# Splitting the last weight but one of a soft MoE into a whole part and two column halves, on one Trainium2 core

## The chip, the core and the metric

The kernel runs on one NeuronCore of a Trainium2 chip. Its engines are the tensor engine (PE, with its weight loads shown apart as PEld), the vector engine (DVE), the scalar engine (ACT), GpSimd (POOL) and the sync engine (SP); 16 DMA engines move data between HBM and the on-chip memory SBUF. Products land in PSUM, which has eight banks. The metric is the time of one execution on the device, in microseconds (us); smaller is better. The time given for a kernel is the median of several executions.

## What is computed

A masked attention over 4 batches, 8 heads, 768 positions and 64 values per head feeds a soft mixture of experts with 8 experts of 4 slots each. The reference, cut to what matters:

```python
scores = np.where(mask, q @ k.T / np.sqrt(64), -1e9)      # per batch and head
x = softmax(scores) @ v                                    # -> (3072, 512)
logits = x @ phi                                           # (3072, 32)
d = softmax(logits, axis=0)
slot_input = (d.T @ x).reshape(8, 4, 512)
for e in range(8):
    slot_out[e] = np.maximum(slot_input[e] @ w1[e], 0) @ w2[e]   # w1: 512x1024, w2: 1024x512
c = softmax(logits, axis=1)
out = c @ slot_out.reshape(32, 512)                        # (3072, 512) float32
```

Half of the heads see all earlier positions, the others the first 4 and the last 64.

## The kernel before

**Loads.** All inputs but three small pieces are loaded by DMAs that POOL issues and that cast float32 to bfloat16 on the way (the helper `dma`, lines 343 to 351; the instruction is at line 347). They go into one queue, q0 in the profile, one behind the other. The weights are called w0 to w15: w0 to w7 are the eight matrices of the first layer, w8 to w15 those of the second, one for each expert. Each is 2 MB as float32 and 1 MB as bfloat16. A matrix of the second layer lies in SBUF as 128 partitions times 8 rows (`fo`) of 512 columns. w8 to w13 arrive whole, in runs of four rows, 4096 bytes as bfloat16, for a partition. w14 and w15 (experts 6 and 7) go by `load_half` (line 395) in two column halves each, so that a run is one row of 256 columns, 512 bytes: w14 left, w15 left, w14 right, w15 right, in this order (lines 967 to 970). They land in memory that the attention has left: `pt` for w14, `qk` for w15, as `qk` for w11, `vx` for w12 and `xv` for w13 (lines 955 to 959).

**Attention.** Sixteen steps (4 batches of 4 pairs of heads) of score products (line 656), exponentials on ACT (line 726), masks on DVE (line 672), products with v (line 800), normalisation (line 824) and transposes; then logits and slot inputs.

**Experts.** `H` (line 1008) multiplies the slot inputs with the first layer, `HR` (line 1018) applies the ReLU, `TH` and `HE` (lines 1030 and 336) transpose. `w2_op` (line 1041) issues for one expert the products W2 (line 1046), one for each of the 8 rows `fo`, on a quarter of the PE array each; all experts add up in one PSUM bank. Experts 0 to 5 take all 512 columns at a time. For experts 6 and 7 the left 256 columns come first and the right 256 after them. Three products with zeros (`wait_zeros`, line 1061, called ZT0 and ZT1) stand between the two experts of a half and keep PE running.

**Output.** `SO.0` and `SO.1` (line 1104) evict the left and the right half of the experts' sum. The 3072 output rows are six groups `gi` of 512, each a tile of 128 partitions, 4 rows `r` and 512 columns. `out_tile` (line 1116) makes one product (OM, line 1121) and one eviction (OE, line 1129 on ACT or 1131 on DVE) for a group, an `r` and a range of columns; the eviction scales with `rrow`, the reciprocal of the row sums. The row sums are 12 small products for three groups at a time (`RW0` and `RW1`, line 1087), and DVE takes their reciprocal (line 1091). The twelve tiles of groups 0 to 2 are made in halves: all left halves as soon as `SO.0` is done, then all right halves after `SO.1`. The twelve tiles of groups 3 to 5 are made whole, after these.

**Stores.** `store` (line 1137, instruction at line 1140). Four stores of left halves go by POOL, on the queue of the loads, behind all of them: 128 KB, 384 KB, 512 KB and 512 KB. SP issues seven more on its own queue, q1: the right halves of group 0 in two pieces of 256 KB, those of groups 1 and 2 (512 KB each), and the three whole groups (1024 KB each).

**Order.** A planner (`Plan.run`, line 69) places all operations by estimated costs and by keys (due times), and the instructions are emitted in that order. What an operation costs in this plan, the DMAs' `took` of line 349 among it, decides the order on each engine and nothing else: at run time each engine goes through its own list and waits on semaphores.

```python
    for e in range(NE - NSPLIT):
        w2_op(e, 0, 2)
    whole = w2o[0]
    for c in range(2):
        for e in range(NE - NSPLIT, NE):
            w2_op(e, c, c + 1)
            if e == NE - 2:
                wait_zeros(f"ZT{c}", 3, kt + (29.5 + e if c else 22.5), w2o[c], c == 0)
```

Of the kernel before, what the change touches and what calls it, by code (L numbers as in the profile page):

```python
# [151 lines left out]
def pe(ns, n=1):  # L152
    occ = ns * n / 1000.0
    return {"PE": (occ, occ + 0.27)}
# [72 lines left out]
def kernel(  # L227
# [15 lines left out]
    B, H, S, D = q.shape  # L243
# [3 lines left out]
    NE, DM, F = moe_w1.shape  # L247
# [61 lines left out]
    def tr_bf(s, n):  # L309
# [19 lines left out]
    def on(eng, occ, late=0.18):  # L329
        return {eng: (occ, occ + late)}  # L330
# [12 lines left out]
    def dma(name, nbytes, buf, dst, src, deps=()):  # L343
        if len(chain) >= 8:
            deps = list(deps) + [chain[-8]]
        iss = pl.op("issue " + name, on("POOL", 0.645, 1.4), -100, deps=list(deps) + [fifo[0]],
                    acq=[buf] if buf else [], lead=1.3, emit=lambda o: nc.gpsimd.dma_start(dst(), src))  # L347
        fifo[0] = iss
        took = nbytes / (395000.0 if nbytes == 1 << 20 and name != "w0" else 423000.0)
        chain.append(pl.op("land " + name, {"DMA": (took, took + 1.85 + 0.05 * len(chain))}, -100, deps=[iss] + chain[-1:], lead=5.2))  # L350
        return chain[-1]

# [23 lines left out]
    NW, NSPLIT = 2 * NE, 2  # L376
    wbuf = [Buf("S8") for _ in range(NW)]
    wland = [None] * NW
    late_mem = {}
# [6 lines left out]
    def w_row(i, x):  # L386
        n = 2 if i < NE else 4
        return w_mem(i)[:, x // n, :].rearrange("p (a f) -> p a f", a=n)[:, x % n, :]

    def w_half(i, c):  # L390
        return late_mem[i]()[:, 2048 * c:2048 * (c + 1)].rearrange("p (a f) -> p a f", a=8)

    hland = {}

    def load_half(i, c, deps=()):
        src = moe_w2[i - NE].rearrange("(fi fo) d -> fi fo d", fo=8)[:, :, 256 * c:256 * (c + 1)]
        hland[i, c] = dma(f"w{i}.{c}", 1 << 20, None, lambda: w_half(i, c), src, deps=deps)

    def load_w(i, deps=()):
        if i == 0:  # L400
# [106 lines left out]
    for x in range(5):  # L507
# [26 lines left out]
    def phi_t2(o):  # L534
        for n in range(4):
# [14 lines left out]
    def load_tile(ti):  # L550

        tbuf[ti], tland[ti], p0 = Buf("S8"), [], 0
        for x, b, x0, x1 in TILES[ti]:
# [8 lines left out]
                  emit=lambda o, x=x: nc.gpsimd.tensor_copy(w_mem(0)[:, 0, KB * x:KB * (x + 1)],  # L562
                                                            w0f[:, KB * x:KB * (x + 1)])) for x in range(4)]
# [116 lines left out]
    for b in range(B):  # L680
        for n in range(4):
            p = 4 * b + n
# [4 lines left out]
            def emit_v2(o, n=n, tr=tr):  # L687
                t = tr_bf(tr.slot, 768)
                for j in range(6):
                    nc.tensor.transpose(t[:, 128 * j:128 * (j + 1)], vT[:, 6 * n + j, :], ident)  # L690

            a = pl.op(f"V2.{p}", pe(56, 6), k0 + 1.5, deps=evs("v", b, n), acq=[tr], rel=[VTb[b]],
                      emit=emit_v2, mode="full", mm=6)

            def emit_vb(o, b=b, n=n, tr=tr):
# [4 lines left out]
                           acq=[VBb[b]] if n == 0 else [], rel=[tr], emit=emit_vb)  # L700
            VFb[p] = Buf("VF")

            def emit_vf(o, b=b, n=n, p=p):
# [4 lines left out]
                           emit=emit_vf)  # L708

            PTb[b, n] = Buf("PT")  # L710
            for kk, g in enumerate(range(5)):
                sc = Buf("SC")
                key = k0 + kk * T / 5.3

                def emit_qk(o, b=b, n=n, g=g, sc=sc):
                    parts, c = [], 0
                    for j, q0, nb in PGROUPS[g]:
# [4 lines left out]
                a = pl.op(f"QK.{p}.{g}", on("PE", 0.235, 0.26), key - 2.0, deps=evs("q", b, n) + evs("k", b, n),  # L722
                          acq=[sc], rel=[QTb[b], KTb[b]], emit=emit_qk, mode="r64", mm=2 * len(PGROUPS[g]))

                def emit_ex(o, b=b, n=n, g=g, sc=sc):
# [12 lines left out]
        for ns in ([(0, 1), (2, 3)] if b == 0 else [(0, 1, 2, 3)]):  # L738
            sc = Buf("SC")

            def emit_lx(o, b=b, sc=sc, ns=ns):
                sc_mms(sc, b, [(128 * x, n, 5, 5, 1) for x, n in enumerate(ns)])

            key = T * (4 * b + ns[0]) + 0.9 * T
            a = pl.op(f"QX.{b}.{ns[0]}", on("PE", 0.06 * len(ns), 0.26), key - 2.0,
                      deps=list(dict.fromkeys(e for n in ns for x in "qk" for e in evs(x, b, n))),
                      acq=[sc], rel=[QTb[b], KTb[b]], emit=emit_lx, mode="r64", mm=2 * len(ns))

            def emit_ex2(o, b=b, sc=sc, ns=ns):
# [4 lines left out]
            e = pl.op(f"EXX.{b}.{ns[0]}", on("ACT", 0.12 + 0.213 * len(ns)), key - 1.0, deps=[a, PTXb[b].op],  # L754
                      acq=[PTXb[b]] if ns[0] == 0 else [], rel=[sc], emit=emit_ex2)

            def emit_mx(o, b=b, ns=ns):
# [5 lines left out]
                      emit=emit_mx)  # L763
# [4 lines left out]
    xto, lgo, elo, dso, eto, tee = {}, {}, {}, {}, {}, {}  # L768
    for b in range(B):
# [164 lines left out]
        if b == B - 1:  # L934
# [29 lines left out]
    load_w(12, deps=[pv_ops[f"PV.{p}.5"] for p in range(8, 12)])  # L964
    load_w(13, deps=[pv_ops["DS.2"]] + [pv_ops[f"XT.{p}"] for p in range(8, 12)] +
           [pv_ops[f"V2.{p}"] for p in range(12, 16)])
    load_half(14, 0, deps=[pv_ops["PV.14.5"]])
    load_half(15, 0, deps=qk_done[3])
    load_half(14, 1)
    load_half(15, 1)  # L970
# [68 lines left out]
    w2o = {}  # L1039

    def w2_op(e, c0, c1):
        def emit_w2(o):
            e4, g0 = e // 4, e % 4
            for fo in range(8):
                g = fo % 4
                nc.tensor.matmul(banks[so.slot][32 * g:32 * (g + 1), 256 * c0:256 * c1],
                                 hT_t[e4][:, fo, 32 * g0:32 * (g0 + 1)], w_row(NE + e, fo) if c1 - c0 == 2 else w_half(NE + e, c0)[:, fo, :],
                                 start=(e == 0 and fo < 4), stop=(e == NE - 1 and fo >= 4),
                                 tile_position=(0, 32 * g), skip_group_check=True)

        land = [wland[NE + e]] if c1 - c0 == 2 else [hland[NE + e, c0]]
        o = pl.op(f"W2.{e}" + ("" if c1 - c0 == 2 else f".{c0}"), on("PE", 0.22 * (c1 - c0), 0.27),
                  kt + (29 + e if c0 == 1 else 16 + e),
                  deps=[hte[e // 4]] + land + [w2o[c] for c in range(c0, c1) if c in w2o],
                  acq=[so] if e == 0 else [], emit=emit_w2, mode="c32", mm=8)
        for c in range(c0, c1):
            w2o[c] = o

# [2 lines left out]
    def wait_zeros(name, n, key, dep, first=False):  # L1061
        def emit_z(o):
            for _ in range(n):
                nc.tensor.matmul(banks[zw.slot][:, 0:448], ident, zt, start=True, stop=True)

        pl.op(name, pe(190, n), key, deps=[dep], acq=[zw] if first else [], rel=[zw], emit=emit_z, mode="full", mm=n)

    for e in range(NE - NSPLIT):
        w2_op(e, 0, 2)
    whole = w2o[0]  # L1070
    for c in range(2):
        for e in range(NE - NSPLIT, NE):
            w2_op(e, c, c + 1)
            if e == NE - 2:
                wait_zeros(f"ZT{c}", 3, kt + (29.5 + e if c else 22.5), w2o[c], c == 0)

    def out_lhs(gi, r):
        return expT[:, r, 128 * gi:128 * (gi + 1)]
# [2 lines left out]
    for x, (g0, g1) in enumerate(((0, 3), (3, 6))):  # L1081
        rw = Buf("BK")

        def emit_rw(o, g0=g0, g1=g1, rw=rw):
            for gi in range(g0, g1):
                for r in range(4):
                    nc.tensor.matmul(banks[rw.slot][:, 4 * gi + r:4 * gi + r + 1], out_lhs(gi, r), cols,
                                     start=True, stop=True)

        def emit_rr(o, g0=g0, g1=g1, rw=rw):  # L1090
            nc.vector.reciprocal(rrow[:, 4 * g0:4 * g1], banks[rw.slot][:, 4 * g0:4 * g1])

        key = kt + (38.5 if x else 21.4)
        a = pl.op(f"RW{x}", pe(29, 4 * (g1 - g0)), key, deps=[eto[b] for b in range(B)] + [o_st, w2o[1] if x else whole],
                  acq=[rw], rel=[], emit=emit_rw, mode="full", mm=4 * (g1 - g0))
        a = pl.op(f"RWR{x}", on("DVE", 0.16), key, deps=[a], rel=[rw], emit=emit_rr)
        for gi in range(g0, g1):
            o_rw[gi] = a
# [38 lines left out]
    def store(eng, m, gi, r0, r1, cs, key):  # L1137
        def emit_st(o):
            dst = out[512 * gi:512 * (gi + 1), :].rearrange("(p r) d -> p r d", r=4)
            (nc.gpsimd if eng == "POOL" else nc.sync).dma_start(dst[:, r0:r1, cs], ot_view(gi)[:, r0:r1, cs])  # L1140

        pl.op(f"ST.{m}.{gi}.{r0}", on(eng, 0.7), key, deps=[oe[m, gi, r] for r in range(r0, r1)], emit=emit_st)
# [8 lines left out]
    for gi, n in halved:  # L1151
        for r in range(n):
            out_tile("r", gi, r, 1, 2, kt + 40 + 0.1 * (4 * gi + r))
        for r0, r1 in [(0, 2), (2, 4)] if gi == 0 else [(0, n)]:
            store("SP", "r", gi, r0, r1, slice(256, 512), kt + 41 + gi + 0.1 * r0)
    for gi in range(6):
        n = dict(halved).get(gi, 0)
        for r in range(n, 4):
# [54 lines left out]
```

## Time and profile before

| | |
|---|---|
| time, median of 3 executions | 147.97 us |
| lowest and highest | 147.84 and 148.62 us |
| the profiled execution's own time | 148.91 us |
| its span, from the first to the last instruction | 147.1 us |
| mean granted PE clock in it | 0.968 of full speed |
| HBM read and written | 52.49 MB and 6.29 MB |

The profile shows one execution. Between its span and its own time lie 148.91 - 147.1 = 1.81 us at start and end that no engine's instruction fills, and the profiled execution is 0.94 us above the median. The first part of the page gives the engines' shares and the third the DMA queues:

```profile
PE 119.7 (81%) x2107; PEld 79.2 (54%) x2107; DVE 111.0 (75%) x254; ACT 107.9 (73%) x147; POOL 42.0 (29%) x75
q0 software_dynamic: 11472, 27.27, 94.1%
q1 hardware_dynamic: 2322, 5.83, 10.5%
```

In the first line stand the busy microseconds of an engine, its share of the span and its number of instructions. In the others stand packets, megabytes (as written, so bfloat16 for a casting load), and the time of the packets as a share of 16 engines' span.

### The profile page before, as it was taken

The page shows a single profiled execution, that of the slowest core. Times are in us where ns is not written, and L with a number is a line of the kernel's source. Part 1 is how long each engine was busy: PE and PEld are TensorE (multiplying, and loading weights), DVE is VectorE, ACT ScalarE, POOL GpSimd, SP SyncE. Part 2 cuts the span into 40 slices and gives each one's busy share as a digit, 9 for nine tenths or more (in the row PEclk, how much of TensorE's full clock was granted, in tenths as well). Part 3 has the DMA queues.
Part 4 walks back from the last instruction along what each step waited for, and adds up shares of the span by engine and source line. Part 5 has one row for each costly group of instructions (what it writes and reads, how often), then busy time and mean ns, then how long its engine had stood idle before and what let it go on. Part 6 is the DMA issues. An engine that isn't in the chain of part 4 may idle for free.

```text
span 147.1 us, 4879 instructions
## 1 busy us (share of the span) xinstructions
PE 119.7 (81%) x2107; PEld 79.2 (54%) x2107; DVE 111.0 (75%) x254; ACT 107.9 (73%) x147; POOL 42.0 (29%) x75
## 2 busy tenths in 40 slices
PE   0167988999989999999999999999959899879000
PEld 0045666677776657776558766666745445443000
DVE  1786299999999999999799899999973312549500
ACT  3152689999999997999998999999971460649200
POOL 6988631120311380100170011405380000340000
PEclk9999999999999999999999999999995999999965
DMA  5999999999999999999999999999999999989995
GB/s 147 270 207 212 217 213 214 213 215 211 216 215 214 212 215 214 217 214 214 215 215 217 214 215 214 214 214 215 214 214 214 206 196 197 168 309 347 404 423 212
DMA packets 13815, 33.40 MB, mean 227 GB/s; under 512 B 802, under 2 KB 6562, under 8 KB 13282
## 3 DMA queue, kind: packets, MB, share of 16 engines
q0 software_dynamic: 11472, 27.27, 94.1%
q1 hardware_dynamic: 2322, 5.83, 10.5%
q8 instruction: 16, 0.26, 0.6%
q14 instruction: 5, 0.04, 0.1%
HBM read 52.49 MB, written 6.29 MB: 400 GB/s over the span
## 4 chain that ended last, share of the span: by engine, by line
PE 27%; DVE 26%; DMA 18%; ACT 15%; issue 5%; POOL 1%; SPq 0%; DVEq 0%; ACTq 0%; POOLq 0%
DMA qk<-in_moe_w_dram 14%; ACT pt L726 11%; PE sc L656 6%; DVE pt L672 5%; PE pv L800 5%; DVE xv L824 5%; DMA phf<-in_moe_phi_dram 4%; DVE qk L336 4%; PE tr L604 3%; PE tr L630 3%; PE bk L1121 2%; PE tr L863 2%; DVE xv L336 2%; DVE slot L1131 2%; DVE vf L705 2%
## 5 line engine op out<-in xcount | busy, mean ns | idle before, releaser
L726 ACT ACTIVATE pt<-sc 128x1024 bf16<-128x1024 f32 x80 | 77.0, 1047 | 3.0 <-PE sc L656 2.8
L656 PE MATMUL sc<-qk 64*128 64x512 bf16 (+3 forms) x256 | 31.4, 311 | 1.2 <-ACT pt L726 0.8
L672 DVE TENSOR_TENSOR pt<-pt,msk 128x1024 bf16<-128x1024 bf16 (+1 forms) x48 | 29.0, 610 | 2.0 <-ACT pt L726 1.8
L800 PEld LDWEIGHTS <-pt 128*128 128x128 bf16 x640 | 23.4, 98 | 6.2 <-issue 5.2
L800 PE MATMUL pv<-vx,pt 128*128 128x65 bf16 x320 | 25.6, 193 | 0.3 <-DVE xv L824 0.2
L800 PE MATMUL pv<-vf,pt 128*128 128x65 bf16 x320 | 21.3, 195 | 0.9 <-DVE xv L824 0.9
L347 POOL DMA_DIRECT2D slot<-in_moe_w_dram x11 | 7.7, 696 | 40.0 <-PE tr L630 34.3
L336 DVE COPY qk<-tr 128x768 bf16<-128x768 bf16 (+2 forms) x33 | 15.1, 482 | 2.1 <-PE tr L604 1.8
L630 PE MATMUL tr<-ident,slot 128*64 128x128 bf16 (+1 forms) x448 | 16.3, 219 | 0.4 <-ACT qk L334 0.3
L824 DVE TENSOR_TENSOR xv<-pv,rs 128x768 bf16<-128x768 f32 (+1 forms) x17 | 15.5, 911 | 0.6
L630 PEld LDWEIGHTS <-slot 128*64 128x64 bf16 (+1 forms) x448 | 13.1, 109 | 5.1 <-issue 4.8
L656 PEld LDWEIGHTS <-qk 64*128 64x128 bf16 x256 | 10.4, 94 | 9.6 <-issue 3.3
L887 POOL COPY expT<-eT 128x192 bf16<-128x192 bf16 x12 | 7.4, 667 | 12.5 <-ACT eT L870 12.5
L1131 DVE TENSOR_SCALAR slot<-bk,rrow 128x256 f32<-128x256 f32 (+1 forms) x19 | 9.2, 562 | 2.2 <-PE bk L1121 2.2
L336 DVE COPY xv<-tr 128x512 bf16<-128x512 bf16 (+2 forms) x20 | 8.0, 410 | 2.5 <-PE tr L604 2.2
L836 PE MATMUL tr<-ident,xv 128*128 128x128 bf16 x96 | 8.4, 224 | 1.3 <-DVE xv L824 0.9
L604 PEld LDWEIGHTS <-slot 96*64 96x64 bf16 x192 | 6.8, 141 | 4.3 <-issue 4.0
L604 PE MATMUL tr<-ident_u,slot 96*64 96x96 bf16 x192 | 7.9, 248 | 1.6 <-DVE phi L544 1.1
L336 DVE COPY xT<-tr 128x768 bf16<-128x768 bf16 (+1 forms) x14 | 7.5, 539 | 1.1 <-PE tr L836 1.1
L1129 ACT ACTIVATE slot<-bk,rrow 128x256 f32<-128x256 f32 (+1 forms) x17 | 7.7, 570 | 0.9 <-PE bk L1121 0.9
L690 PE MATMUL tr<-ident,xv 128*128 128x128 bf16 x96 | 8.1, 220 | 0.0
L1140 POOL DMA_DIRECT2D out_dram<-slot x4 | 2.9, 714 | 17.7 <-DVE slot L1131 17.6
(121 smaller groups left out, 165.6 us busy)
## 6 DMA issues: line engine op xcount, KB each, us to landing
slot<-in_moe_w_dram POOLq DMA_DIRECT2D x10, 1024.0 KB, 24.6
out_dram<-slot SPq DMA_DIRECT2D x3, 1024.0 KB, 5.9
slot<-in_q_dram POOLq DMA_DIRECT2D x2, 768.0 KB, 19.9
slot<-in_k_dram POOLq DMA_DIRECT2D x2, 768.0 KB, 23.8
qk<-in_moe_w_dram SPq DMA_DIRECT2D x1, 1024.0 KB, 6.3
slot<-in_v_dram POOLq DMA_DIRECT2D x2, 512.0 KB, 21.5
qk<-in_moe_w_dram POOLq DMA_DIRECT2D x1, 1024.0 KB, 17.4
vx<-in_moe_w_dram POOLq DMA_DIRECT2D x1, 1024.0 KB, 21.5
```

The costliest lines, as they stand in the source:

```text
L336: nc.vector.tensor_copy(dst, src)
L347: acq=[buf] if buf else [], lead=1.3, emit=lambda o: nc.gpsimd.dma_start(dst(), src))
L604: nc.tensor.transpose(t[64 * i:64 * (i + 1), :, :, s, :], rv[:, i, 8 * c + s, :], ident_u)
L630: nc.tensor.transpose(t[64 * i:64 * (i + 1), :, s, :], rv[:, i, 8 * c + s, :], ident[0:R, 0:R])
L656: nc.tensor.matmul(scb[sc.slot][:, i, c:c + 128 * nb], kk, qq.rearrange("p b c -> p (b c)"), start=True, stop=True)
L672: nc.vector.tensor_tensor(pT, pT, mh, op=ALU.mult)
L690: nc.tensor.transpose(t[:, 128 * j:128 * (j + 1)], vT[:, 6 * n + j, :], ident)
L726: nc.scalar.activation(pTs[PTb[b, n].slot][:, :, 512 * g:512 * (g + 1)], scb[sc.slot], ACT.Exp, scale=scale)
L800: nc.tensor.matmul(pvb[:, bk, c:c + 65], lt, rhs, start=(j == 0), stop=(j == i))
L824: nc.vector.tensor_tensor(xo, pvw[:, :, :, 0:64], r.rearrange("p i (j o) -> p i j o", o=1).to_broadcast([P, 2, i1 - i0, 64]), op=ALU.mult)
L836: nc.tensor.transpose(t[:, 128 * i:128 * (i + 1)], xv[:, i, 128 * n:128 * (n + 1)], ident)
L1131: nc.vector.tensor_scalar(d, banks[bf.slot][:, 0:w], sc_, None, op0=ALU.mult)
```

## The change

w14 is cut differently. Its rows `fo` 0 to 3 are loaded whole, 512 columns, by a new DMA (`load_whole`, view `w_whole`: 128 runs of 4096 bytes), and its rows 4 to 7 in two column halves of 512 KB float32 each. The order of the last loads becomes: w14 whole part, w14 left, w15 left, w14 right, w15 right, five DMAs for four. `w2_op` runs expert 6 three times, with four products each: rows 0 to 3 on all columns, rows 4 to 7 on the left, rows 4 to 7 on the right. The first row sums (`RW0`) depend on the left product of expert 7 and not on the last whole product, and the key goes from 21.4 to 23.5; ZT1's key goes from 35.5 to 33.0. The right stores of groups 1 and 2 move from SP to POOL. The plan's rate of a DMA is chosen by a flag in its byte count.

In the built program PE's list is the same up to the experts. From there it differs so, in this order: w14's whole part (4 products), w14 left (4), ZT0, w15 left (8), RW0 (12 small products), the twelve left OM, w14 right (4), ZT1, w15 right (8), RW1, the right OM. Before, RW0 stood ahead of w14 left, and w14 left and right had 8 products each. DVE's reciprocal of RW0 stands ahead of the left evictions as before. POOL's list ends with the four left stores and, behind these, the two right ones.

```diff
-        took = nbytes / (395000.0 if nbytes == 1 << 20 and name != "w0" else 423000.0)
+        took = nbytes / (395000.0 if nbytes & 1023 else 423000.0)
...
     def w_half(i, c):
+
+        if i < NW - 1:
+            return late_mem[i]()[:, 2048 + 1024 * c:3072 + 1024 * c].rearrange("p (a f) -> p a f", a=4)
         return late_mem[i]()[:, 2048 * c:2048 * (c + 1)].rearrange("p (a f) -> p a f", a=8)
+
+    def w_whole():
+        return late_mem[NW - 2]()[:, 0:2048].rearrange("p (a f) -> p a f", a=4)
...
     def load_half(i, c, deps=()):
         src = moe_w2[i - NE].rearrange("(fi fo) d -> fi fo d", fo=8)[:, :, 256 * c:256 * (c + 1)]
-        hland[i, c] = dma(f"w{i}.{c}", 1 << 20, None, lambda: w_half(i, c), src, deps=deps)
+        if i < NW - 1:
+            src = src[:, 4:]
+        hland[i, c] = dma(f"w{i}.{c}", (1 << 20) - 100 if i == NW - 1 else (1 << 19) - 100, None, lambda: w_half(i, c), src, deps=deps)
+
+    def load_whole(i, deps):
+        src = moe_w2[i - NE].rearrange("(fi fo) d -> fi fo d", fo=8)[:, 0:4]
+        wland[i] = dma(f"w{i}", 1 << 20, None, w_whole, src, deps=deps)
...
-    load_half(14, 0, deps=[pv_ops["PV.14.5"]])
+    load_whole(14, deps=[pv_ops["PV.14.5"]])
+    load_half(14, 0)
     load_half(15, 0, deps=qk_done[3])
     load_half(14, 1)
     load_half(15, 1)
...
     def w2_op(e, c0, c1):
+        part = e == NE - 2
+        fos = range(8) if not part else range(4) if c1 - c0 == 2 else range(4, 8)
+
         def emit_w2(o):
             e4, g0 = e // 4, e % 4
-            for fo in range(8):
+            for fo in fos:
                 g = fo % 4
...
-    for e in range(NE - NSPLIT):
+    for e in range(NE - 1):
         w2_op(e, 0, 2)
-    whole = w2o[0]
     for c in range(2):
         for e in range(NE - NSPLIT, NE):
             w2_op(e, c, c + 1)
             if e == NE - 2:
-                wait_zeros(f"ZT{c}", 3, kt + (29.5 + e if c else 22.5), w2o[c], c == 0)
+                wait_zeros(f"ZT{c}", 3, kt + (27.0 + e if c else 22.5), w2o[c], c == 0)
...
-        key = kt + (38.5 if x else 21.4)
-        a = pl.op(f"RW{x}", pe(29, 4 * (g1 - g0)), key, deps=[eto[b] for b in range(B)] + [o_st, w2o[1] if x else whole],
+        key = kt + (38.5 if x else 23.5)
+        a = pl.op(f"RW{x}", pe(29, 4 * (g1 - g0)), key, deps=[eto[b] for b in range(B)] + [o_st, w2o[x]],
...
         for r0, r1 in [(0, 2), (2, 4)] if gi == 0 else [(0, n)]:
-            store("SP", "r", gi, r0, r1, slice(256, 512), kt + 41 + gi + 0.1 * r0)
+            store("SP" if gi == 0 else "POOL", "r", gi, r0, r1, slice(256, 512), kt + 41 + gi + 0.1 * r0)
```

More of the change, by code (lines that the diff above doesn't have):

```diff
@@ L1041, in w2_op @@
     def w2_op(e, c0, c1):
+        part = e == NE - 2
+        fos = range(8) if not part else range(4) if c1 - c0 == 2 else range(4, 8)
         def emit_w2(o):
             e4, g0 = e // 4, e % 4
-            for fo in range(8):
+            for fo in fos:
                 g = fo % 4
+                if c1 - c0 == 2:
+                    rhs = w_whole()[:, fo, :] if part else w_row(NE + e, fo)
+                else:
+                    rhs = w_half(NE + e, c0)[:, fo - 4 if part else fo, :]
                 nc.tensor.matmul(banks[so.slot][32 * g:32 * (g + 1), 256 * c0:256 * c1],
-                                 hT_t[e4][:, fo, 32 * g0:32 * (g0 + 1)], w_row(NE + e, fo) if c1 - c0 == 2 else w_half(NE + e, c0)[:, fo, :],
+                                 hT_t[e4][:, fo, 32 * g0:32 * (g0 + 1)], rhs,
                                  start=(e == 0 and fo < 4), stop=(e == NE - 1 and fo >= 4),
@@ L1051, in w2_op @@
         land = [wland[NE + e]] if c1 - c0 == 2 else [hland[NE + e, c0]]
-        o = pl.op(f"W2.{e}" + ("" if c1 - c0 == 2 else f".{c0}"), on("PE", 0.22 * (c1 - c0), 0.27),
+        o = pl.op(f"W2.{e}" + ("" if c1 - c0 == 2 else f".{c0}"), on("PE", 0.22 * (c1 - c0) * len(fos) / 8, 0.27),
                   kt + (29 + e if c0 == 1 else 16 + e),
                   deps=[hte[e // 4]] + land + [w2o[c] for c in range(c0, c1) if c in w2o],
-                  acq=[so] if e == 0 else [], emit=emit_w2, mode="c32", mm=8)
+                  acq=[so] if e == 0 else [], emit=emit_w2, mode="c32", mm=len(fos))
         for c in range(c0, c1):
```

## The prediction

> **What bounds the kernel now.** First I read the page's span and its strip of 40 slices: are the DMA engines ever idle?
>
> ```profile
> span 147.1 us, 4879 instructions
> DMA  5999999999999999999999999999999999989995
> ```
>
> Hardly, so the kernel is a stream of transfers, and the question is what the change does to it at the end. Second, the last loads: POOL's own timeline says when each was issued, the view of DMA issues how long it took to land.
>
> ```profile
> 93.15 0.71 POOL L347 DMA_DIRECT2D vx<-in_moe_w_dram  x1 [0.19 <-ACT vx L751]
> 103.28 0.70 POOL L347 DMA_DIRECT2D xv<-in_moe_w_dram  x1
> 106.31 0.90 POOL L347 DMA_DIRECT2D pt<-in_moe_w_dram  x1 [2.33 <-PE pv L800]
> 107.20 0.88 POOL L347 DMA_DIRECT2D qk<-in_moe_w_dram  x1
> 108.07 0.88 POOL L347 DMA_DIRECT2D pt<-in_moe_w_dram  x1
> 108.94 0.88 POOL L347 DMA_DIRECT2D qk<-in_moe_w_dram  x1
> 127.37 2.96 POOL L1140 DMA_DIRECT2D out_dram<-slot  x4 [17.56 <-DVE slot L1131]
> ...
> vx<-in_moe_w_dram POOLq DMA_DIRECT2D x1, 1024.0 KB, 21.5
> xv<-in_moe_w_dram POOLq DMA_DIRECT2D x1, 1024.0 KB, 16.2
> pt<-in_moe_w_dram POOLq DMA_DIRECT2D x1, 512.0 KB, 15.8
> qk<-in_moe_w_dram POOLq DMA_DIRECT2D x1, 512.0 KB, 17.6
> pt<-in_moe_w_dram POOLq DMA_DIRECT2D x1, 512.0 KB, 19.4
> qk<-in_moe_w_dram POOLq DMA_DIRECT2D x1, 512.0 KB, 21.2
> ```
>
> Issue plus landing time, in the order of the rows: w12 landed at 114.65, w13 at 119.48, w14 left at 122.11, w15 left at 124.8, w14 right at 127.47, w15 right at 130.14. Issue ran more than ten microseconds ahead, so the queue never lacked work. Third, what happened on PE, ACT and DVE around the two halves (the timeline):
>
> ```profile
> 125.31 0.40 PE L1046 MATMUL bk<-qk,xT 128*32 128x256 bf16 x8
> 125.76 0.47 ACT L1104 ACTIVATE msk<-bk,rcs 128x256 bf16<-128x256 f32 x1 [4.38 <-PE bk L1046]
> 126.29 2.01 PE L1121 MATMUL bk<-msk,expT 128*128 128x256 bf16 x12 [0.58 <-ACT msk L1104]
> 126.59 2.44 DVE L1131 TENSOR_SCALAR slot<-bk,rrow 128x256 f32<-128x256 f32 x6 [1.96 <-PE bk L1121]
> ...
> 128.22 0.40 PE L1046 MATMUL bk<-pt,xT 128*32 128x256 bf16 x8
> 128.56 0.74 PE L1064 MATMUL bk<-zt,ident 128*128 128x448 bf16 x3
> 130.15 0.40 PE L1046 MATMUL bk<-qk,xT 128*32 128x256 bf16 x8 [0.84 <-DMA qk<-in_moe_w_dram]
> 130.48 0.45 PE L1087 MATMUL bk<-cols,expT 128*128 128x1 bf16 x12
> 130.59 0.47 ACT L1104 ACTIVATE msk<-bk,rcs 128x256 bf16<-128x256 f32 x1 [1.59 <-PE bk L1046]
> 130.97 0.23 DVE L1091 RECIPROCAL rrow<-bk 128x12 f32<-128x12 f32 x1 [1.93 <-PE bk L1087]
> 131.12 4.89 PE L1121 MATMUL bk<-msk,expT 128*128 128x256 bf16 x24 [0.19 <-ACT msk L1104]
> 131.43 0.48 DVE L1131 TENSOR_SCALAR slot<-bk,rrow 128x256 f32<-128x256 f32 x1 [0.22 <-PE bk L1121]
> 132.09 6.53 SPq L1140 DMA_DIRECT2D out_dram<-slot  x7
> ```
>
> The left product of w15 starts at 125.31, some 0.5 us after its data; the right one waits for its data until 130.15. The chain of waits that ended last closes with evictions, at 136.90 + 1.32 = 138.22:
>
> ```profile
> 136.90 1.32 DVE slot L1131 x2
> ```
>
> Last, the windows (length, busy time of PE, PEld, DVE, ACT and POOL, granted PE clock, DMA share, GB/s):
>
> ```profile
> 127.50:128.00 0.50, 0.47 (x4) 0.28 (x3) 0.50 (x2) 0.50 (x3) 0.45 (x1) 1.00 0.72 93
> 129.00:129.50 0.50, 0.30 (x2) 0.09 (x1) 0.04 (x1) 0.00 (x1) 0.50 (x1) 1.00 0.40 127
> ...
> 128.50:131.00 2.50, 1.58 (x31) 0.81 (x24) 0.57 (x3) 0.91 (x3) 1.82 (x3) 1.00 0.82 266
> 131.00:133.50 2.50, 2.35 (x15) 1.45 (x15) 2.28 (x7) 2.03 (x7) 0.00 (x0) 1.00 1.01 374
> 133.50:137.50 4.00, 2.44 (x11) 0.78 (x8) 4.00 (x8) 3.44 (x6) 0.00 (x0) 1.00 1.04 361
> 137.50:145.00 7.50, 0.00 (x0) 0.00 (x0) 0.71 (x2) 0.00 (x0) 0.00 (x0) 0.74 1.03 426
> ```
>
> The evictions are over at 138.22, but the DMA engines work on until 145 with a share of 1.01 to 1.04: from 131 on there is always a store waiting for them. A bound of bytes, then: what is not stored by 131 must be stored later, and the end follows. Only before 131 do they have idle time: 93 GB/s at 127.5, and a share of 0.40 at 129, while the last load is still landing (130.14). The 16 engines don't finish the loads together, and those that are done wait for the first stores. **So the end is set by when the left stores begin**, not by the last load, the right half or the evictions.
>
> **Loads: all end 0.25 us earlier.** w13, in 4096-byte runs, took 119.48 - 114.65 = 4.83 us for 2 MB of float32, 2.42 per MB. The 512-byte halves took (130.14 - 119.48) / 4 = 2.67 per MB. One MB changes kind: 2.67 - 2.42 = 0.25 us. The bounds are 0 (the DMA's fifth piece costs what the runs save) and this 0.25; I take 0.25, as the new DMA's runs are w13's. The extra issue is one more piece of 0.70 to 0.90 us on POOL, which does nothing between 109.8 and 127.37; were that cover gone, it would be 0.9 us. New landings: whole part 119.48 + 2.42 = 121.9; w14 left + 1.33 = 123.2; w15 left + 2.67 = 125.9; w14 right 127.2; w15 right 129.9.
>
> **The left half: 0.6 us later.** w15 left now has 2.5 MB ahead of and in it instead of 2 MB: its data come at 125.9, not 124.8. PE started 0.5 us after them before, and that slack is eaten first. PE isn't late itself: RW0 (0.45, the row of RW1) has gone from ahead of ZT0, and w14's 16 products have become eight ahead of it. So PE waits for the data and starts at 125.9, 0.6 us later than 125.31. Bounds: 0.5 (the landing times have one decimal) to 0.85 (the whole part at 2.67).
>
> **RW0 behind the left product: nothing.** The right half shows the same pattern already: product at 130.15, RW1 0.33 later, `SO.1` on ACT 0.44 later, reciprocal from 0.82 to 1.05, first OM at 0.97, first eviction at 1.28. In the left half, where RW0 stood ahead, OM began 0.98 and the eviction 1.28 after the product. RW0 lies under `SO.0`, the reciprocal under the first OM, with 0.2 us to spare; without that cover the price is RW0 and its reciprocal, 0.45 + 0.23 us.
>
> **PE between the halves: nothing.** The left evictions shift to 127.2 until 129.65, w14 right to 128.85 with half its products, ZT1 (0.74) ends near 129.8, w15 right's data are there at 129.9. It is close; if ZT1 is late by 0.2 us, `SO.1` is late by 0.2. That would cost nothing either: the right stores aren't awaited (next part). ACT and DVE are free for `SO.1` at 130.35.
>
> **Left stores: 0.6 us later, paid in full.** POOL issues the four back to back, 2.96 us from 127.37, each with its wait already met but for the first. They shift together, to 128.0 until 131.0. The share of 0.40 at 129 says what was missing there: stores to do, not engines, so the 0.25 us that the loads gain doesn't make up for it. At the 374 GB/s that follow, 0.6 x 374 = 224 KB are not stored by 131 and have to be stored later; the share is 1.01 and more from then on, and the end moves by 0.6 us. Bounds: 0, if the last engine to finish the loads sets the end (rival 1), and 0.85.
>
> **Right stores: about nothing.** Two rows for the meeting of the queues, the issue of the fourth left store and the landing times of the left four, and one for the first right store:
>
> ```profile
> 129.59 0.74 POOL L1140 DMA_DIRECT2D out_dram<-slot  x1
> ...
> DMA to landing us min/median/max: 3.1/3.7/4.5
> ...
> out_dram<-slot SPq DMA_DIRECT2D x1, 256.0 KB, 2.7
> ```
>
> Before, the last left store landed at 129.59 + 4.5 = 134.1 and the first right one at 132.09 + 2.7 = 134.8, one behind the other. Now the left ones last until 134.7, and the right one could land at 134.55: the queues overlap, and the right half has nothing to be late for. Groups 1 and 2 on POOL: POOL is free from 131.0, their tiles come from 133 on; two issues of 0.75. On SP nothing waits behind them any more, but the three whole stores need evictions that end when they did, and there is a backlog. What is left is the rate. The nearest rows are 374 GB/s (POOL's stores of 1 KB runs, 131 to 133.5) and 361 (SP's, 133.5 to 137.5): 1.05 MB take 2.8 instead of 2.9 us, a gain of 0.1. Ends: 426, with two queues as fast as whole rows, 2.46 us, a gain of 0.45; 266, 3.95 us, a loss of 1.05. I take the gain of 0.1.
>
> The Trainium skill, "DMA: Bandwidth & Descriptors", section "Issuing engines are not separate DMA queues", says that DMAs of all issuers run on the same 16 engines and that several issuers only save issue time. By that rule the move is worth 0, and the sum would be 0.6 instead of 0.5; the trace before, where the left stores end as the right ones begin, can't show it.
>
> **Sum.** 0.6 - 0.1 = +0.5 us. Against the profiled execution: span 147.1 -> 147.6, own time 148.91 -> 149.4. That execution was 0.94 us above the median, 147.97, so for the median 148.5 us.
>
> **The rivals.**
>
> 1. *The lateness is hidden.* If the slowest DMA engine, done with w15 at 130.14, sets the end, then it is busy from there without a gap, and the loads' 0.25 us pass to the end: 147.97 - 0.25 = 147.7. For it: it is the last to be free, and all engines must finish. Against it: the others wait for stores at 129, with a share of 0.40, and while they wait it catches up.
> 2. *Two queues fill the engines.* Then the 4.0 us at 361 GB/s go at 426: 4.0 x 361 / 426 = 3.4, a gain of 0.6. With the left half late by 0.6 this is 148.0; with rival 1 as well, 147.97 - 0.25 - 0.6 = 147.1. For it: whole rows reach 426 on the same engines. Against it: the share is over 1.0 at 361 already, so the small runs themselves cost the time.
> 3. *The casting queue is slow for the right stores.* POOL writes descriptors while DVE evicts, and if the two stores go at 266 GB/s as from 128.5 to 131, they take 1.05 us longer; with +0.6, 149.6. It decides only if the whole stores can't fill the gaps. Against it: three of the four left issues ran beside DVE's evictions, and all four together took 2.96 us.
> 4. *Nothing of the load is gained* (0 for 0.25): w15 left lands 0.25 later, and the end is 0.25 worse than the forecast, 148.7.
>
> **How the numbers follow.** Forecast, with rival 4 as its upper edge, 55%: 148.2 to 148.9. Rival 1 or 2 alone, 147.6 to 148.1, 22%. Both, about 147.1, 9%. Rival 3, 149 to 149.6 as it costs a half or all of its 1.05 us, 14%. The range 147.5 to 149.2 leaves out the first end and most of the other, some 20%. What a measurement of this kernel can tell from no change is about 0.5%, 0.74 us: below 147.23 is faster, above 148.71 slower. Faster: both first rivals, and a little, 0.12. Slower: rival 3 and the upper part of the forecast, where its bounds of 0.85 for the left half and 0 for the loads lie, 0.14 + 0.32 = 0.46. The rest, 0.42, is within.
>
> **What would show it.** Loads right: w15 right's product near 129.9. Left right: w15 left's product at 125.9 with a wait for the DMA ahead of it, and the first left store at 128.0. If the first left store is there before 127.6, the forecast is wrong from the start. Bound right: from 131.6 to 145 a DMA share of 1.0 and a rate near 400 GB/s, and the last bytes half a microsecond later; a rate above 400 between 133.5 and 137.5 is rival 2, a rate below 340 or a share below 0.95 there is rival 3. If the span is shorter although the left stores are later, then the bound of bytes from 131 is wrong, and rival 1 or 2 holds.

## The result, and the profile after

| | before | after |
|---|---|---|
| median of 15 executions each | 148.56 us | 149.04 us |
| lowest and highest | 147.84 and 149.25 | 148.70 and 149.89 |
| profiled execution: own time, span | 148.91, 147.1 | 148.91, 147.1 |
| mean granted PE clock in it | 0.968 | 0.956 |

The ratio after to before is 1.0051, with a 95% interval of 1.0032 to 1.0071: 0.76 us slower (0.48 to 1.05). The forecast was +0.5 us, less than the 0.5% (0.74 us) that the prediction took as the least that can be told from no change, with a chance of 0.46 for slower than that and 0.42 for within it; the kernel is slower by 0.02 us more than that. The median of the three executions shown with the kernel before, 147.97, is the second lowest of its fifteen, and the two profiled executions are equally long by chance, so neither pair of numbers may be compared alone: differences inside a profile count, and the ratio.

The timeline of the changed kernel: start, length, engine, line, operation; in brackets the idle time ahead of it and what ended that.

```profile
125.13 0.40 PE L1066 MATMUL bk<-qk,xT 128*32 128x256 bf16 x8 [1.71 <-DMA qk<-in_moe_w_dram]
128.62 1.30 PE L1084 MATMUL bk<-zt,ident 128*128 128x448 bf16 x3
129.85 0.62 PE L1066 MATMUL bk<-qk,xT 128*32 128x256 bf16 x8
...
127.19 2.95 POOL L1159 DMA_DIRECT2D out_dram<-slot  x4 [18.79 <-DVE slot L1150]
133.96 1.49 POOL L1159 DMA_DIRECT2D out_dram<-slot  x2 [3.81 <-DVE slot L1150]
...
131.36 6.79 DVE L1150 TENSOR_SCALAR slot<-bk,rrow 128x256 f32<-128x256 f32 x13 [0.21 <-PE bk L1140]
...
132.02 6.53 SPq L1159 DMA_DIRECT2D out_dram<-slot  x5
```

The left product of w15 now waits 1.71 us for its data, where PE was at work without a pause before. From w13's landing (118.63 by the trace's DMA records) to this product it is 6.50 us, before 125.31 - 119.48 = 5.83: 0.67 later, where the forecast said 0.6. w13 itself landed 0.85 us earlier in this execution, its slowest engine being 2.5 us behind the first for 3.5, so the clock times don't show it. Landing on 0.67 is in part luck: over the five profiles whose left half is untouched the same distance is 5.34 to 6.07 us.

The windows of the same kernel, with the columns of the prediction's:

```profile
128.50:131.00 2.50, 2.38 (x27) 0.84 (x24) 0.44 (x2) 0.90 (x3) 1.63 (x3) 0.54 0.83 279
131.00:133.50 2.50, 2.42 (x15) 1.45 (x15) 2.29 (x7) 2.03 (x6) 0.00 (x0) 1.00 0.99 358
133.50:137.50 4.00, 2.37 (x10) 0.78 (x8) 4.00 (x8) 3.36 (x6) 1.42 (x2) 1.00 0.88 334
...
135.00:135.50 0.50, 0.50 (x2) 0.10 (x2) 0.50 (x2) 0.50 (x2) 0.45 (x1) 1.00 0.55 229
...
136.40:136.90 0.50, 0.00 (x0) 0.00 (x0) 0.50 (x2) 0.46 (x1) 0.00 (x0) 1.00 0.73 254
```

Between 133.5 and 137.5 the DMA share is 0.88 with 334 GB/s, before 1.04 with 361. This is the sign that the prediction gave for its third rival (a share below 0.95, a rate below 340): just where the two moved stores are due, the DMA engines run dry, down to 0.55 and 229 GB/s at 135. Before, the same half microseconds were full:

```profile
135.00:135.50 0.50, 0.50 (x3) 0.17 (x2) 0.50 (x2) 0.50 (x2) 0.00 (x0) 1.00 1.07 377
...
136.40:136.90 0.50, 0.00 (x0) 0.00 (x0) 0.50 (x2) 0.50 (x1) 0.00 (x0) 1.00 1.10 387
```

### The profile page after: what moved, and what is told of

It is laid out like the page before. It is cut to its first block, busy times and chain, and to the rows that moved or that the text cites. A ratio compares the mean times of both kernels' runs of the same rounds, so it can differ in the third digit from the quotient of the medians.

```text
span 147.1 us, 4873 instructions
## 1 busy us (share of the span) xinstructions
PE 118.9 (81%) x2103; PEld 78.3 (53%) x2103; DVE 110.9 (75%) x254; ACT 107.7 (73%) x147; POOL 43.7 (30%) x78
## 4 chain that ended last, share of the span: by engine, by line
PE 34%; DVE 21%; DMA 17%; ACT 17%; issue 3%; SPq 0%; DVEq 0%; POOL 0%; ACTq 0%
DMA qk<-in_moe_w_dram 13%; ACT pt L738 12%; PE sc L668 7%; PE pv L812 7%; DVE pt L684 4%; PE bk L1140 4%; DMA phf<-in_moe_phi_dram 4%; DVE qk L336 3%; DVE xv L836 3%; PE tr L642 3%; PE tr L875 3%; PE tr L616 2%; PE tr L848 2%; DVE slot L1150 2%; DVE xv L336 2%
## 5 line engine op out<-in xcount | busy, mean ns | idle before, releaser
L1159 POOL DMA_DIRECT2D out_dram<-slot x6 | 4.3, 710 | 22.8 <-DVE slot L1150 22.6
L616 PE MATMUL tr<-ident_u,slot 96*64 96x96 bf16 x192 | 7.3, 238 | 1.2 <-DVE phi L556 0.8
L616 PEld LDWEIGHTS <-slot 96*64 96x64 bf16 x192 | 6.3, 133 | 3.6 <-issue 3.2
## 6 DMA issues: line engine op xcount, KB each, us to landing
slot<-in_v_dram POOLq DMA_DIRECT2D x2, 512.0 KB, 21.4
```

Of the source, the lines that this page charges most:

```text
L616: nc.tensor.transpose(t[64 * i:64 * (i + 1), :, :, s, :], rv[:, i, 8 * c + s, :], ident_u)
```

## The experiments

Three times are read in each profile: F, the start of the first left store's issue (the POOL row of the stores, or the SP row where SP issues them); R, the start of the right evictions (DVE's row of 13); and L, the landing of the last store, from the trace's records of landings. The table stands here once, and the experiments refer to it. The column "later of two" is the larger of F + 18.45 and R + 14.2. The first constant is L - F of the profile before, the second was read off e6 to e8, so these four rows agree by construction; the others are tests.

| kernel | F | R | L | later of two | L minus it | span end - L |
|---|---|---|---|---|---|---|
| before | 127.37 | 131.43 | 145.82 | 145.82 (F) | 0.00 | 1.28 |
| e1, after with stores on SP | 127.24 | 130.90 | 145.73 | 145.69 (F) | 0.04 | 1.28 |
| e3, w14 split only | 127.01 | 130.36 | 145.50 | 145.46 (F) | 0.04 | 1.28 |
| e5, zeros on the left | 128.15 | 132.02 | 146.56 | 146.60 (F) | -0.04 | 1.28 |
| e6, RW0 behind | 125.98 | 130.52 | 144.65 | 144.72 (R) | -0.07 | 1.28 |
| e7, left stores on SP | 126.93 | 131.53 | 145.74 | 145.73 (R) | 0.01 | 1.04 |
| e8, both of these | 125.73 | 130.48 | 144.68 | 144.68 (R) | 0.00 | 1.04 |
| e11, zeros on the right | 126.34 | 131.66 | 145.82 | 145.86 (R) | -0.04 | 1.28 |
| after | 127.19 | 131.36 | 146.18 | 145.64 (F) | **0.54** | 0.92 |
| e2, two right stores on POOL | 126.89 | 130.70 | 145.69 | 145.34 (F) | **0.35** | 0.92 |
| e4, after with longer zeros | 127.73 | 131.16 | 146.41 | 146.18 (F) | **0.23** | 0.92 |
| e10, four right stores on POOL | 126.25 | 130.78 | 145.95 | 144.98 (R) | **0.97** | 0.91 |
| e9, all stores on POOL | 126.23 | 130.46 | 145.86 | 144.68 (F) | **1.18** | 2.77 |

### One part of the change at a time

e1 is the changed kernel with the two right stores back on SP.

```diff
-            store("SP" if gi == 0 else "POOL", "r", gi, ...
+            store("SP", "r", gi, ...
```

> The changed kernel with its two right stores of groups 1 and 2 back on SP. Late left half (the prediction's theory: it costs 0.6 us, the move gains 0.1): 0.6 us above the kernel before, ratio 1.004. Late right stores (POOL starts them late and the DMA engines run dry around 135 and 136.5): the 0.75 us come back, ratio 0.999 to 1.001, and no window between 133.5 and 137.5 has a DMA share below 0.9. PE clock (the right half is late because PE's clock falls to 0.5 after its long wait): no difference from the changed kernel, ratio 1.005.

Measured: 148.96 us, ratio to before 1.0041 (1.0011 to 1.0071). e2 is the other half, the kernel before with this one move.

> The kernel before with the two right stores of groups 1 and 2 on POOL and nothing else. Late left half: 0.1 us faster, ratio 0.999. Late right stores: 0.4 to 0.75 us slower, ratio 1.003 to 1.005, with a DMA share below 0.8 in a window near 135 and another near 136.7. PE clock: the same, ratio 1.000, as PE's wait of 0.84 us and its clock of 1.0 stay.

Measured: 148.48 us, ratio 1.0021 (0.9987 to 1.0054). e3 is the changed kernel without the move, and with RW0 ahead again (its key 21.4 and its dependence on the last whole product), so that the split of w14 stands alone.

> The changed kernel with the two stores on SP and the first row sums ahead of the left product: of the change, only w14's split is left. Late left half: 0.6 us above the kernel before, ratio 1.004. Late right stores: the split alone costs nothing that can be told, ratio 0.999 to 1.001. PE clock: PE still waits more than 1 us for w15 left, its clock falls, and the ratio is 1.002 to 1.003.

Measured: 149.06 us, ratio 1.0051 (1.0014 to 1.0088). The timeline of e1:

```profile
127.24 3.11 POOL L1159 DMA_DIRECT2D out_dram<-slot  x4 [18.46 <-DVE slot L1150]
...
130.90 6.79 DVE L1150 TENSOR_SCALAR slot<-bk,rrow 128x256 f32<-128x256 f32 x13 [0.23 <-PE bk L1140]
```

The window of e1 in which the two stores are due:

```profile
133.50:137.50 4.00, 1.91 (x8) 0.55 (x6) 4.00 (x7) 2.90 (x6) 0.00 (x0) 1.00 1.05 363
```

The same window of e3:

```profile
133.50:137.50 4.00, 1.38 (x6) 0.29 (x3) 3.65 (x6) 2.37 (x5) 0.00 (x0) 0.96 1.06 369
```

With the stores on SP the engines are full again (1.05 and 1.06 for 0.88), and the last landing follows the first left store by 18.49 us in both, 18.45 before. So the split alone makes the kernel slower by 0.5%, as the forecast's left half says; and the move makes holes in the transfers, which it did not say. By the times alone the move can't be told from nothing: the interval of e2 holds 1. Of the two holes below 0.8 that e2 was expected to show, the first is there, half a microsecond earlier than in the changed kernel; the second is shallower (0.82 from 136.0 to 136.5):

```profile
134.50:135.00 0.50, 0.43 (x3) 0.06 (x1) 0.50 (x2) 0.50 (x2) 0.29 (x1) 1.00 0.67 256
```

e4 asks whether the slower PE clock is to blame. In the changed kernel PE stands still for 1.71 us, and its granted clock falls to 0.54 in the window from 128.5; ZT1 takes 1.30 us for 0.74 and the right product 0.62 for 0.40. Seven more zero products in ZT0 fill the pause.

```diff
-            for _ in range(n):
+            for _ in range(n + 7 if first else n):
```

> The changed kernel with ten products with zeros in ZT0 instead of three, so that PE doesn't idle ahead of w15's left product. Late left half: as the changed kernel, ratio 1.005. Late right stores: as the changed kernel, 1.005, or 0.1 us better. PE clock: the granted clock stays at 1.0 from 127 to 130.5, the right product starts 0.2 us after its data or less, and 0.2 to 0.4 us come back, ratio 1.002 to 1.003.

Measured: 149.23 us, ratio 1.0043 (1.0009 to 1.0078); the 1.002 to 1.003 expected of a slow clock lie in the interval too, so the time alone doesn't decide. The window of e4 after the pause:

```profile
128.50:131.00 2.50, 2.04 (x31) 1.04 (x30) 1.13 (x4) 1.46 (x4) 2.18 (x3) 1.00 0.66 215
```

The clock stays at 1.00 there, and nothing is seen to be won. The traces speak against the slow clock as a cause: in the changed kernel it begins at 127.38, after the first left store was issued (127.19), and F is the later bound; and e3, the split alone, is as slow as the whole change with a clock of 1.00 until 137.

### How late the left half may be, and how late the right

e5 adds the same seven zero products to the kernel before, and so delays the left half and nothing else.

> The kernel before with seven more zero products in ZT0 (10 instead of 3; in the profile before three took 0.74 us, so seven are about 1.4 to 1.7 us), nothing else. The left product of w15 and the first left store move back by that much, the loads not at all. Late left half (the forecast's mechanism): the distance from the first left store to the last landing stays near 18.45 us, the first left store comes at about 128.8 to 129.0, and the time grows by 1.4 us, ratio about 1.009 to 1.010; a little less if DMA engines are still loading at 129. Lateness hidden (rival 1 of the prediction; the last load or the right evictions set the end): the time stays, ratio 1.000 to 1.002, and that distance shrinks to about 17 us.

Measured: 149.40 us, ratio 1.0078 (1.0047 to 1.0109), or 1.16 us (0.70 to 1.62). The timeline of e5:

```profile
124.08 2.06 PE L1064 MATMUL bk<-zt,ident 128*128 128x448 bf16 x10
126.08 0.40 PE L1046 MATMUL bk<-qk,xT 128*32 128x256 bf16 x8
...
128.15 2.95 POOL L1140 DMA_DIRECT2D out_dram<-slot  x4 [19.17 <-DVE slot L1131]
```

Ten zeros take 2.06 us, three took 0.74: 1.32 us of delay, and the end comes 18.41 us after the first left store. F itself is 128.15, not 128.8 to 129.0, as it differs from one execution to the next. Rival 1 of the prediction, lateness hidden, falls: it gives 0.

e11 does the same to the right half: nine more zero products in ZT1.

```diff
-            for _ in range(n):
+            for _ in range(n if first else n + 9):
```

> The kernel before with nine more zero products in ZT1 (12 instead of 3, by the 2.06 us that ten took in e5 about 1.8 us more), nothing else: ZT1, which ended 0.84 us before the data of w15 right, ends about 1 us after them, and the right product, the right evictions and all SP stores come about 1.0 us later; the left half and the loads stay. The prediction's step: the right half has nothing to be late for, a store is always waiting, ratio 1.000 to 1.001. Second bound: over the nine profiles so far, with right stores on SP, the end follows the later of two times, first left store + 18.4 and start of the right evictions + 14.2 (in the profile before 145.8 and 145.6), so that only 0.2 us of lateness are hidden: the end moves by about 0.8 us, ratio 1.005 to 1.006.

Measured: 148.95 us, ratio 1.0045 (1.0024 to 1.0066). The timeline of e11:

```profile
128.00 2.44 PE L1064 MATMUL bk<-zt,ident 128*128 128x448 bf16 x12
130.37 0.40 PE L1046 MATMUL bk<-qk,xT 128*32 128x256 bf16 x8
...
126.34 2.96 POOL L1140 DMA_DIRECT2D out_dram<-slot  x4 [17.43 <-DVE slot L1131]
...
131.66 6.78 DVE L1131 TENSOR_SCALAR slot<-bk,rrow 128x256 f32<-128x256 f32 x13 [0.23 <-PE bk L1121]
```

The window of e11 that holds R:

```profile
131.00:133.50 2.50, 2.28 (x21) 1.44 (x18) 2.08 (x6) 2.03 (x6) 0.00 (x0) 1.00 0.73 268
```

The right product starts 0.42 us after its data (129.95 by the DMA records), the DMA engines run dry before the right stores come (a share of 0.73; before, with the left stores 1.03 us later, 1.01), and the end stands 19.48 us after the first left store. **The right half is awaited too.** R + 14.2 was read off e6, e7 and e8 (14.13, 14.21, 14.20); e11 was expected at the later of the two bounds before it ran, and came out 0.04 us from it. The time grew by 0.67 us (0.36 to 0.98), a little less than expected, and not by the 0 to 0.15 us of the prediction's step. In the profile before the two bounds are 145.82 and 145.63: the right half has 0.2 us to spare, and in an execution whose left half comes earlier it has none.

### RW0, and the left stores on SP

e6 is the kernel before with RW0 behind the left product, as the change has it. e7 is the kernel before with `store("SP", "l", ...)` for the four left stores. e8 has both.

> The kernel before with one part of the change alone: RW0 behind the left product of w15 instead of ahead of ZT0; w14 whole in column halves as before, all right stores on SP. In the profile before the left product began 0.5 us after its data had landed, with PE at work without a pause, and RW0 took 0.45 us of that work. Late left half: product and first left store come up to 0.45 us earlier, the end too, ratio 0.997 to 0.998 to the kernel before. Lateness hidden: ratio 1.000. If RW0 and its reciprocal then hold up SO.0 or the first eviction, the first left store does not come earlier by the profile, and the ratio is 1.000 or above for that reason.

> The kernel before with the four left stores issued by SP instead of POOL, nothing else. In the profile before POOL issued the first left store 0.3 us after the eviction that it needs, in the profile after POOL issued the first of the two moved right stores 0.55 us after its tile, while SP issued one 0.06 us after its tile. Slow reaction of the casting queue (the theory for the store move): the first left store is issued 0.25 us earlier, and the time falls by about 0.25 us, ratio 0.998. Rival, the queue does not matter: ratio 1.000. Rival, on another queue than the loads the stores take the DMA engines away from the loads that are still under way: w15 right lands later than 3.9 us after the left product, and the right half with it; by the forecast's bound of bytes this costs nothing, else up to 1 us.

> Both edits of the two runs ahead of this one in the kernel before: RW0 behind the left product, and the left stores on SP. If both gains are real and the first left store sets the end, they add up: 0.45 + 0.25 = 0.7 us, ratio 0.995. If the bound is elsewhere, ratio 1.000.

Measured: e6 148.12 us, ratio 0.9998 (0.9977 to 1.0018); e7 147.90 us, 0.9978 (0.9959 to 0.9996); e8 147.82 us, 0.9972 (0.9957 to 0.9987). The timeline of e8:

```profile
123.87 0.40 PE L1046 MATMUL bk<-qk,xT 128*32 128x256 bf16 x8 [0.60 <-DMA qk<-in_moe_w_dram]
...
130.48 6.78 DVE L1131 TENSOR_SCALAR slot<-bk,rrow 128x256 f32<-128x256 f32 x13 [0.23 <-PE bk L1121]
...
125.73 11.97 SPq L1140 DMA_DIRECT2D out_dram<-slot  x11
```

RW0's place is worth nothing measurable. In e6 and e8 the product waits for its data, and R is the later bound, so an earlier left half gains nothing. On SP the first left store follows the left product by 1.86 us in e8, on POOL by 2.06 in e6: 0.20 us. The loads don't suffer from the second queue: in e7 w15 right landed 5.37 us after w15 left (before 5.35). The expectation's figure of 3.9 us, counted from the left product, was wrong (4.79 in the profile before), so that part of it tells nothing; and e7 was expected at 0.998 for the earlier first store, but in its profile F comes 2.05 us after the product (before 2.06), PE being at half clock there, and the end of the span is nearer to L instead (last column: 1.04 for 1.28).

That column has a plain reading in the instruction records. At the end SP waits for each store's semaphore in turn, some 0.06 us each, in a fixed order. Before, six more waits stand behind that of the store that lands last (S[109]); in e7 and e8 two do; in the changed kernel none does, S[118] being the last in line:

```
before  145.839 S[109]  145.898 S[111]  145.960 S[114]  146.019 S[115]  146.081 S[116]  146.140 S[117]  146.202 S[118]
after   143.755 S[117]  146.199 S[118]
```

So moving two stores to another queue shortens the close of the kernel by some 0.36 us, for no reason that has to do with the transfers. e8 beats both kernels, by 0.28% the one before.

### More stores on POOL

e10 puts the four right stores of the kernel before on POOL (`store("POOL", "r", ...)`), e9 these and the three whole ones.

> The kernel before with the four right stores on POOL, the three whole ones on SP as before. Late casting queue: the loss of e9 or a little less, since the whole stores, issued by SP without delay, can fill a gap from about 135 on: ratio 1.002 to 1.004, distance 18.7 to 19.0 us. If the loss in the changed kernel comes from the whole stores being mixed with the moved right ones (the right store of group 2 took 6.6 us to land there), then this run shows it and e9, where one queue keeps them in order, does not. The queue does not matter: 1.000.

> The kernel before with all seven remaining stores (four right, three whole) on POOL too; SP stores nothing. Late casting queue: POOL issued the first moved store 0.55 us after its tiles in the profile after, where SP took 0.06 us, and the DMA engines ran dry for it; with four right stores instead of two the loss is at least that of e2 (0.2 to 0.5 us), since the first right store is late by 0.25 to 0.55 us and nothing is there to fill the gap: ratio 1.002 to 1.005, the distance from the first left store to the last landing 18.8 to 19.2 us against 18.45, and a DMA share below 0.95 between 131 and 137.5. The queue does not matter (rule of the Trainium skill, as the prediction cites it): ratio 1.000, distance 18.45.

Measured: e10 148.60 us, ratio 1.0028 (1.0005 to 1.0051); e9 150.64 us, 1.0175 (1.0142 to 1.0208). The windows of e10:

```profile
131.00:133.50 2.50, 2.50 (x12) 1.45 (x11) 2.50 (x7) 2.27 (x6) 1.54 (x3) 0.50 0.75 272
133.50:137.50 4.00, 2.71 (x11) 0.95 (x9) 3.84 (x7) 3.56 (x6) 1.31 (x2) 0.90 0.90 321
```

The same windows of e9, and below them those of e8, whose R is the same as e9's (130.48 and 130.46) and whose stores are all on SP:

```profile
131.00:133.50 2.50, 2.47 (x14) 1.11 (x13) 2.50 (x7) 2.50 (x7) 1.86 (x3) 1.00 0.86 305
133.50:137.50 4.00, 1.47 (x6) 0.35 (x4) 3.74 (x6) 2.47 (x5) 2.08 (x4) 1.00 0.90 319
...
131.00:133.50 2.50, 2.47 (x14) 1.11 (x13) 2.50 (x7) 2.50 (x7) 0.00 (x0) 1.00 0.88 308
133.50:137.50 4.00, 1.49 (x6) 0.37 (x4) 3.76 (x6) 2.48 (x5) 0.00 (x0) 1.00 1.06 385
```

Both lose about a microsecond of transfer time (0.97 and 1.18 in the table, where two moved stores lost 0.23 to 0.54). The second window shows it: 0.90 in both, 1.06 in e8. The first doesn't: e8 is nearly as dry there (0.88) as e9 (0.86). By the DMA records the first packet of a right store starts 2.33 us after R in e9 and in e10, and 1.61 and 1.59 us after it in e6 and e11, where SP issues the right stores: 0.7 us of the loss is this later start. A mixing of whole and right stores is not the reason, since in e9 one queue keeps them in order. Nor is the PE clock of 0.50 in e10's first window: e6 has it there too and loses nothing.

e9's other 1.5 us, with which it lies far above the expected 1.002 to 1.005, are at the close: by the instruction records POOL drains for 10.1 us from 137.76, where its last issue begins, until 147.87, 2.0 us after the last store has landed. In the changed kernel the drain at POOL's last issue ended at 143.1, hidden. The sum for e9, 1.18 + 2.77 - 1.28 = 2.67 us, is near the measured 1.75% of 148.18, 2.60.

## Why the prediction was off, point by point

**The loads, 0.25 us earlier: 0.18, and not for the last engine.** The 16 engines finish w15 right spread over 2.5 to 3.8 us, and executions differ in when the stream starts, so both ends have to be counted from w13's. From the first engine's end of w13 to the first engine's end of w15 right it is 10.44 us in all four kernels with the split and 10.62 in all nine without: 0.18 us, nearer to the forecast than to rival 4. From w13's landing to w15 right's, the last engine's ends, it is 10.60 in e1 and e3, and 10.62 to 10.64 in all kernels without the split but e11 (11.01): next to nothing.

**The left half, +0.6 us, paid in full: right.** The data of w15 left landed 6.46 to 6.47 us after w13 with the split and 5.25 to 5.31 without, 1.2 later for a forecast of 1.1. Over several profiles, F is 127.37, 126.89, 126.25, 126.23 and 126.34 where the left half is untouched (before, e2, e10, e9, e11; mean 126.62) and 127.19, 127.24 and 127.01 with the split (after, e1, e3; mean 127.15), 0.53 later. The times of e3 and e1 give 0.76 us (0.21 to 1.30) and 0.61 us (0.16 to 1.05), and e5 shows that a delay is paid. The prediction's own sign against it, a first left store before 127.6, did come (127.19); but F differs by 1.14 us among kernels with an untouched left half, so a fixed clock time could not tell.

**RW0, nothing: right** (e6). **PE between the halves, nothing:** it holds for the time, though not as described: ZT1 took 1.30 us at half clock, and the right product began 0.19 us after its data.

**Right stores, "about nothing", taken at -0.1 us: this step failed.** Its reason was that the queues overlap, that there is a backlog, and that "the right half has nothing to be late for". The backlog is small. In the profile before, SP issues its first right store at 132.09, and its first packet starts at 133.51, just as the last packet of the left stores does (133.52). In e6 and e11 it took 0.95 and 0.93 us from this issue to the first packet, so before, the store stood in line for some 0.5 us; by the two bounds the right half has 0.2 us to spare. A right store that is later than that is a hole in the transfers, and POOL's are.

In the trace of the changed kernel the tiles of group 1 are evicted by 133.41, POOL issues at 133.96, and the store's first packet starts at 135.24. SP's packets of group 0 have all started by 134.96, so the engines run dry at 135. Before, SP issued the same store at 133.54, after an eviction that ended at 133.48, and its queue was not empty yet. The second hole, at 136.4, ends with the first packet of SP's next store, at 136.93, 1.35 us after its issue; before, SP's queue had no such pause.

The loss up to the last landing is 0.23 to 0.54 us in three profiles and grows with the stores moved (e10, e9). What hid it from the times is the close of the kernel, 0.36 us shorter by SP's fewer waits; what is left, -0.1 to +0.2 us by the table (0.54 - 0.36 and 0.23 - 0.36), agrees with the +0.31 us of e2 (-0.19 to +0.80) and can't be told more closely. In the prediction's own terms it is nearest to rival 3, at a quarter to a half of its price, together with a gain that no rival had. But rival 3 spoke of a slow rate, and what the runs show is a late start: between the two holes, from 135.5 to 136.5, the engines move 401 to 410 GB/s. Why POOL starts later is not shown.

Of the rivals, 1 falls (e5), and 2 too: the rate from 133.5 was 334 GB/s, not 426.

The Trainium skill, "DMA: Bandwidth & Descriptors", section "Issuing engines are not separate DMA queues", gave the move 0, and the net time doesn't contradict it; the landings, 0.23 to 0.54 us later, do, since the queue decides when the transfer starts. Its section "Issuing engine by pattern" names Sync for simple loads and stores, and this the runs bear out: from the end of the first left eviction to the store's issue it is 0.29 us on POOL (before) and 0.09 us on SP (e7), and from there to its first packet 1.15 and 0.85 us.

**The sum.** The split alone gave 0.76 us (e3), the change without the move 0.61 (e1), the whole change 0.76 (0.48 to 1.05). The forecast's 0.5 lies in that interval too. Of the quarter of a microsecond that it lacks, 0.1 is the gain of the right stores, which no run shows: in its place the profiles have a net -0.1 to +0.2. The rest is up to 0.16 us in the left half, into which the loads' missing 0.07 goes. The shares stay open within these intervals.

## What to carry to other kernels

A DMA share of 1.0 in a window of several microseconds doesn't prove a backlog: delay one producer on purpose (a few products with zeros are enough) and see whether the end follows. Where two streams of work feed the same engines, each has its own bound, and the slack of the second is what a change of the first can gain at most: here 0.2 us. Before a store goes to another queue, look at how soon that queue starts, whether its last store is the last to land, and which wait stands last at the close.

## What the runs showed of the hardware that was not expected

- POOL's drain, which begins with its last DMA issue, ended 1.7 to 2.0 us after POOL's last store had landed, in all eleven profiles in which POOL stores. Only in e9, where that store is the last of all, did it set the end of the kernel.
- SP's waits at the close cost 0.06 us each, also for stores that landed long ago: the store that lands last is best waited for last.
- From the issue of the first left store to its first packet POOL took 1.15 us in all eleven profiles, SP 0.85 in e7 and e8.
- Behind 115 us, pauses of 1.28 to 1.75 us on PE were followed by a granted clock of 0.50 for 3.4 us in five kernels (after, e1, e6, e7, e10), beginning 0.2 to 2.3 us after the pause ended; in e8, a pause of 1.30 us was not, and in two (before, e5) the clock fell near 110 us without such a pause.
